# Larger first loads of q and k, and the identity matrix filled on another engine, in an attention and feed-forward kernel

## The chip, the cores and the metric

The kernel runs on one core of one Trainium2 chip. A core has five engines with a queue of instructions each: TensorE (PE, with its weight loads as PEld), VectorE (DVE), ScalarE (ACT), GpSimd (POOL) and SyncE (SP). Each works through its queue in order and waits at an instruction whose inputs are not there yet. The metric is the device time of one execution in microseconds; less is better. A profile shows one execution, with times counted from the start of its span.

## What is computed

Attention without a softmax (squared ReLU in its place), then a gated feed-forward block. Batches 8, heads 12, sequence 448, head size 64; model width 768, inner width 1536; everything is float32 outside.

```python
def _attn_ref(q, k, v):
    S = q.shape[2]
    scale = 1.0 / np.sqrt(q.shape[-1])
    scores = scale * np.matmul(q, k.transpose(0, 1, 3, 2))
    attn = np.maximum(scores, 0.0) ** 2 / S
    return np.matmul(attn, v)

def _moe_ref(x, w_gate, w_val, w_out):     # x: the heads side by side, 3584 rows
    g = x @ w_gate
    gelu = 0.5 * g * (1.0 + erf(g / np.sqrt(2.0)))
    return (gelu * (x @ w_val)) @ w_out
```

## The kernel before

Every load from DRAM of q, k, v and the weights is issued by GpSimd and casts float32 to bfloat16 on the way. For each batch, q lies on partitions 0 to 63 of one tile, qk16, and k on partitions 64 to 127, so one pass of TensorE transposes both. load_qk (line 205, its DMA on line 214) loads q or k of a batch for heads h0 to h1; load_v (line 220, DMA on line 227) loads v in two halves.

A group m holds four heads, that is two pairs. Of the first two batches TensorE makes the transposes (add_transposes, matmuls on line 377, with the identity matrix ident as the other operand), 14 matmuls for a pair of heads. VectorE copies the result from PSUM to SBUF (line 381). From batch 2 on, DMA transposes on SP's queue do this. Then, for a group, seven score tiles follow (add_scores): matmuls on line 162, a relu on ScalarE (line 425), and its square on VectorE (line 431). Two PSUM tiles hold scores, so a score tile waits for the relu of the tile two before it. add_values multiplies with v (line 162 again) and VectorE scales the result into xT (line 487). add_gate_value and add_out are the feed-forward block: gate and value matmuls, a Gelu on ScalarE (line 552), the product on VectorE (line 557), and the output matmuls, whose results are copied (line 613) and stored from SP's queue.

In the texts, T0, T1, T2 and so on are the transposes of the first batch's pairs of heads, in order.

The order of the work comes from a planner at build time (run_plan, line 23). TensorE's work is split into PE0 and PE1, for the two row halves of its array, and both go into TensorE's one queue. PE0's order is fixed: all its items are sorted by due times written in the code. PE1, ACT, DVE and SP each take the item that can start first by the plan, where every item has a cost and a delay, and a load has an arrival time from its bytes and a rate (300 bytes per nanosecond for the first batch). POOL's order is the order in which the code lists it. Where the plan leaves TensorE idle in its first 30 us, fill (line 328) sets filler matmuls on a tile of zeros (line 340). Ten pairs of warm-up matmuls on the same zeros (line 762) stand at the very front.

PE0 of the first batch begins thus: warm-up, T0, scores 1 and 2, T1, scores 3 to 6, T2, score 7, score 8, first values, score 9, T3, and so on.

The identity is made on GpSimd by make_identity, behind the first loads of q and k: a memset of the 128x128 tile to zero (masks.py line 197) and then an affine select that puts ones on the diagonal (masks.py line 199). The zero tile warm and a small table are set on VectorE ahead of all planned work, and ScalarE runs one Gelu on that table.

Of the kernel before, what the change touches and what calls it, by code (L numbers as in the profile page):

```python
# [88 lines left out]
def kernel(  # L89
# [10 lines left out]
    nc = tc.nc  # L100
# [43 lines left out]
    psX = []  # L144

    ident = const.tile([128, 128], bf16)
    warm = const.tile([128, 512], bf16)
    nc.vector.memset(warm[:, :], 0.0)

# [19 lines left out]
    ACT, DVE, POOL, SP, IDLE = [], [], [], [], []  # L169
# [35 lines left out]
    def load_qk(b, i, h0, h1, deps=()):  # L205

        src = (q, k)[i]

        def tile_of():
            if b not in qk16:  # L210
                qk16[b] = qkv.tile([128, H * S // P * D], bf16, name="qk16", tag="qk16")
            return qk16[b][HALF[i], :]

        op = load(4 * (h1 - h0) * S * D, lambda: nc.gpsimd.dma_start(  # L214
            tile_of().rearrange("p (h x) -> p h x", h=H)[:, h0:h1, :],
            src[b, h0:h1].rearrange("h (p c) d -> p h (c d)", c=SC)), deps, rate=400e3 if b else 300e3)
        for pr in range(h0 // 2, h1 // 2):
            head_op[b, pr, i] = op

    def load_v(b, h0, h1, deps=()):  # L220

        for i in range(2):
            def emit(i=i):
                if b not in v16:
                    v16[b] = qkv.tile([128, H, VC, D], bf16, name="v16", tag="v16")
                c0 = i * (SC - VC)
                return nc.gpsimd.dma_start(  # L227
                    v16[b][HALF[i], h0:h1, :, :],
                    v[b, h0:h1].rearrange("h (p c) d -> p h c d", c=SC)[:, :, c0:c0 + VC, :])
            op = load(4 * (h1 - h0) * VC * P * D, emit, deps, rate=400e3 if b else 300e3)  # L230
            for pr in range(h0 // 2, h1 // 2):
                head_op[b, pr, 2 + i] = op
# [405 lines left out]
        then(at, step, *ops, cp)  # L638


    for h0, h1 in ((0, 2), (2, 4), (4, 8), (8, 12)):
        load_qk(0, 0, h0, h1)
        load_qk(0, 1, h0, h1)
        if h0 == 0:
            POOL.append(Op("POOL", 0.6, lambda: make_identity(nc, ident)))
        if h0 > 2:
            load_v(0, h0 - 4, h1 - 4)
    load_v(0, 8, 12)
    load_w12(0)
# [148 lines left out]
```

## Time and profile before

| | us |
|---|---|
| median of 5 runs | 423.94 |
| lowest, highest | 423.51, 426.0 |
| the profiled execution | 423.61 |
| its span in the profile | 421.8 |
| ScalarE busy in the span | 223.9 |
| VectorE busy in the span | 214.0 |
| GpSimd busy in the span | 73.6 |

The profiled execution is 1.8 us longer than its span, which begins with the first recorded instruction. The granted TensorE clock is 0.999 of full speed. The first instructions of GpSimd's queue, by its timeline:

| start us | GpSimd instruction |
|---|---|
| 1.25, 1.95 | q and k, heads 0 and 1 |
| 2.54, 2.85 | identity: memset, affine select |
| 3.09, 3.67 | q and k, heads 2 and 3 |
| 4.27, 4.88 | q and k, heads 4 to 7 |
| 5.48 | v, heads 0 to 3, two issues |
| 6.68, 7.28 | q and k, heads 8 to 11 |
| 7.88 | v, heads 4 to 7, two issues |
| 9.50, 11.36 | v, heads 8 to 11 |
| 12.06, 12.89 | first slices of the gate and value weights |

In a line of a timeline stand the start, the duration, the engine, the line of the code, the operation, what it writes and reads with shapes, how many instructions were merged, and in brackets how long the engine had been idle and what ended that. In a table by stages stand the stretch, its length, and the busy time and number of instructions of each engine. Sizes of DMAs are those of the stored side, which is half of what is read here.

### The profile page before, as it was taken

The numbers are of one execution on the slowest core, as the hardware profiler recorded it, in microseconds if no ns is written. First come the engines' busy times: TensorE is split into PE (matmuls) and PEld (weight loads), VectorE is DVE, ScalarE is ACT, GpSimd is POOL, SyncE is SP. The second block draws the span as 40 slices with busy tenths as digits, with TensorE's granted clock in tenths as the row PEclk, the third lists the DMA queues.
The fourth block names the chain that finished last, engine by engine and source line by source line (L and its number), as shares of the span: only waits on it lengthen the run. The fifth ranks groups of instructions, "written<-read, shape, count | busy, mean of one in ns | idle before, by whom it ended". The sixth has DMA issues, their size and how long they took to land.

```text
span 421.8 us, 19605 instructions
## 1 busy us (share of the span) xinstructions
PE 415.1 (98%) x9087; PEld 371.2 (88%) x9090; DVE 214.0 (51%) x347; ACT 223.9 (53%) x320; POOL 73.6 (17%) x120
## 2 busy tenths in 40 slices
PE   8999999999999999999999999999999999999996
PEld 3558768777998999999999889999999989999995
DVE  3876665266655665356544566456643655212201
ACT  4956663377655655555646555565555556222220
POOL 8655400122022131002300122011310000000000
PEclk9999999999999999999999999999999999999999
DMA  7999997779599899736974299635974100220034
GB/s 102 193 199 198 200 209 123 138 82 126 86 150 172 103 120 116 156 47 74 144 138 104 39 100 145 132 65 66 143 130 97 40 2 3 51 67 3 2 79 113
DMA packets 75281, 44.91 MB, mean 106 GB/s; under 512 B 36160, under 2 KB 71744, under 8 KB 75200
## 3 DMA queue, kind: packets, MB, share of 16 engines
q0 software_dynamic: 37152, 24.39, 43.6%
q1 hardware_dynamic: 37888, 19.08, 25.2%
q8 instruction: 71, 1.16, 1.1%
q10 hardware_dynamic: 160, 0.20, 0.1%
q14 instruction: 10, 0.08, 0.1%
HBM read 48.76 MB, written 11.01 MB: 142 GB/s over the span
## 4 chain that ended last, share of the span: by engine, by line
PE 96%; DMA 1%; POOL 1%; ACT 0%; issue 0%; DVE 0%; POOLq 0%
PE ff L162 86%; PE sp L162 8%; DMA qk<-in_k_dram 1%; PE sp L377 1%; POOL qk L214 1%; PE ff L377 1%; ACT rl L425 0%; PE ff L340 0%; DVE qkT L381 0%; DVE attnT L431 0%; DVE osb L613 0%; POOL ident masks.py:199 0%; POOL ident masks.py:197 0%; POOLq L782 0%
## 5 line engine op out<-in xcount | busy, mean ns | idle before, releaser
L425 ACT ACTIVATE rl<-sp 128x896 bf16<-128x896 f32 x168 | 152.4, 918 | 90.8 <-PE sp L162 81.0
L162 PE MATMUL ff<-xT,wg 64*64 64x448 bf16 x2304 | 196.5, 349 | 0.0
L162 PE MATMUL ff<-xT,wv 64*64 64x448 bf16 x2304 | 195.4, 349 | 0.0
L162 PE MATMUL ff<-wo,uT 64*64 64x384 bf16 (+1 forms) x2736 | 151.4, 320 | 0.0
L431 DVE TENSOR_TENSOR attnT<-rl 128x896 bf16<-128x896 bf16 x168 | 104.0, 623 | 68.9 <-ACT rl L425 66.1
L162 PEld LDWEIGHTS <-wv 64*64 64x64 bf16 x2304 | 124.5, 107 | 9.4 <-issue 0.2
L162 PEld LDWEIGHTS <-wg 64*64 64x64 bf16 x2304 | 123.0, 107 | 10.5 <-issue 0.5
L162 PEld LDWEIGHTS <-uT 64*64 64x64 bf16 x2736 | 128.3, 107 | 4.0 <-issue 0.6
L162 PE MATMUL sp<-qkT 64*64 64x448 bf16 (+1 forms) x768 | 107.5, 328 | 0.8 <-ACT rl L425 0.5
L557 DVE TENSOR_TENSOR uT<-gel,ff 128x448 bf16<-128x448 bf16 x96 | 59.6, 621 | 75.2 <-PE ff L162 66.5
L162 PE MATMUL ff<-attnT,v 64*64 64x448 bf16 (+1 forms) x768 | 88.3, 326 | 0.1
L552 ACT ACTIVATE gel<-ff 128x448 bf16<-128x448 f32 x96 | 52.1, 542 | 48.6 <-PE ff L162 48.0
L162 PEld LDWEIGHTS <-qkT 64*64 64x64 bf16 x768 | 46.3, 106 | 9.9 <-issue 4.0
L613 ACT COPY osb<-ff 128x384 f32<-128x384 f32 x54 | 25.8, 477 | 50.4 <-PE ff L162 50.4
L162 PEld LDWEIGHTS <-v 64*64 64x64 bf16 x768 | 47.7, 107 | 4.2 <-issue 1.1
L487 DVE TENSOR_SCALAR xT<-ff 128x448 bf16<-128x448 f32 x48 | 29.9, 623 | 33.1 <-PE ff L162 33.0
L227 POOL DMA_DIRECT2D v<-in_v_dram x48 | 29.5, 621 | 50.6 <-DVE uT L557 32.5
L214 POOL DMA_DIRECT2D qk<-in_q_dram x25 | 15.5, 622 | 111.3 <-DVE uT L557 105.8
L214 POOL DMA_DIRECT2D qk<-in_k_dram x25 | 15.4, 615 | 65.3 <-DVE uT L557 49.3
L262 DVE COPY qkr<-qk 128x1792 bf16<-128x1792 bf16 x18 | 19.4, 1078 | 0.0
L613 DVE COPY osb<-ff 128x192 f32<-128x192 f32 (+1 forms) x3 | 1.2, 421 | 17.9 <-PE ff L162 17.9
L377 PEld LDWEIGHTS <-qk 128*64 128x64 bf16 x168 | 5.1, 109 | 3.1 <-issue 3.0
(23 smaller groups left out, 41.5 us busy)
## 6 DMA issues: line engine op xcount, KB each, us to landing
out_dram<-osb SPq DMA_DIRECT2D x54, 192.0 KB, 3.0
v<-in_v_dram POOLq DMA_DIRECT2D x48, 128.0 KB, 4.4
qk<-in_q_dram POOLq DMA_DIRECT2D x23, 224.0 KB, 4.9
qk<-in_k_dram POOLq DMA_DIRECT2D x23, 224.0 KB, 4.8
wg<-in_moe_w_gate_dram POOLq DMA_DIRECT2D x6, 384.0 KB, 10.5
wv<-in_moe_w_val_dram POOLq DMA_DIRECT2D x6, 384.0 KB, 11.0
wo<-in_moe_w_out_dram POOLq DMA_DIRECT2D x4, 576.0 KB, 14.9
qkT<-qkr SPq DMA_TRANSPOSE x36, 4.6
```

The source lines that it names most:

```text
L162: return nc.tensor.matmul(o, lhsT, rhs, start=start, stop=stop, tile_position=(P * row, P * col))
L214: op = load(4 * (h1 - h0) * S * D, lambda: nc.gpsimd.dma_start(tile_of().rearrange("p (h x) -> p h x", h=H)[:, h0:h1, :], src[b, h0:h1].re ...
L227: return nc.gpsimd.dma_start(v16[b][HALF[i], h0:h1, :, :], v[b, h0:h1].rearrange("h (p c) d -> p h c d", c=SC)[:, :, c0:c0 + VC, :])
L262: nc.vector.tensor_copy(qkr[b][:, m], qk16[b].rearrange("p (h c d) -> p c h d", c=SC, d=D)[:, :, 4 * m:4 * m + 4])
L377: nc.tensor.transpose(t[HALF[j], c, :], src[:, 2 * (2 * m + r) + j, c, :], ident[:, :], tile_position=(0, P * j))
L425: nc.scalar.activation(rl[:, :, :], box[0][:, :, 0:S], AF.Relu)
L431: nc.vector.tensor_tensor(a[:, :, :], box[1][:, :, :], box[1][:, :, :], op=ALU.mult)
L487: nc.vector.tensor_scalar_mul(xT[b][:, pr, :], box[0][:, 0:S], scalar1=out_scale)
L552: nc.scalar.activation(gel[b, fc][:, :], box[0][:, 0:S], AF.Gelu)
L557: u_op[b, fc].ins = nc.vector.tensor_tensor(uT[b][:, fc, :], gel.pop((b, fc))[:, :], box[0][:, 0:S], op=ALU.mult).ins
L613: cp.ins = (nc.vector.tensor_copy if last else nc.scalar.copy)(osb[t][:, cols], box[0][:, 0:N]).ins
```

## The change

The first batch's q and k are loaded in three steps of four heads instead of two steps of two heads and two of four. The identity's memset moves from GpSimd to VectorE, where it stands ahead of the memset of warm; only the affine select stays on GpSimd, in the same place, behind the first load of q and of k. The first v loads follow the second step, as they did. The planner's cost entry for the identity on POOL goes from 0.6 to 0.4. No other work is added or left out.

```diff
     ident = const.tile([128, 128], bf16)
+    nc.vector.memset(ident[:, :], 0.0)
     warm = const.tile([128, 512], bf16)
     nc.vector.memset(warm[:, :], 0.0)
...
-    for h0, h1 in ((0, 2), (2, 4), (4, 8), (8, 12)):
+    for h0, h1 in ((0, 4), (4, 8), (8, 12)):
         load_qk(0, 0, h0, h1)
         load_qk(0, 1, h0, h1)
         if h0 == 0:
-            POOL.append(Op("POOL", 0.6, lambda: make_identity(nc, ident)))
-        if h0 > 2:
+            POOL.append(Op("POOL", 0.4, lambda: make_identity(nc, ident, nomemset=True)))
+        if h0:
             load_v(0, h0 - 4, h1 - 4)
     load_v(0, 8, 12)
```

With nomemset=True make_identity leaves out its memset and does the rest.

## The prediction

> **What bounds the kernel now.** I read the page first: busy shares, then the chain of waits. TensorE works 98% of the span and the chain is TensorE for 96% of it, so any edit counts only by what it does to the moment at which TensorE's unbroken stretch begins.
>
> ```profile
> span 421.8 us, 19605 instructions
> PE 415.1 (98%) x9087; PEld 371.2 (88%) x9090; DVE 214.0 (51%) x347; ACT 223.9 (53%) x320; POOL 73.6 (17%) x120
> PE 96%; DMA 1%; POOL 1%; ACT 0%; issue 0%; DVE 0%; POOLq 0%
> ```
>
> The change edits the first 12 us of loads. The table by stages says where TensorE stops being gapless (columns: stretch, length, then busy time and count of PE, PEld, DVE, ACT, POOL, granted clock, DMA share, GB/s). Before 30 us it has gaps and from there none to 360 us: what the opening loses or gains reaches the end one for one.
>
> ```profile
> 20.00:25.00 5.00, 4.65 (x66) 2.84 (x64) 5.00 (x10) 5.00 (x7) 2.29 (x4) 1.00 1.37 199
> 25.00:30.00 5.00, 4.85 (x92) 2.89 (x93) 3.36 (x6) 0.43 (x2) 2.64 (x5) 1.00 1.38 199
> 30.00:35.00 5.00, 5.00 (x113) 3.11 (x104) 2.57 (x5) 4.00 (x6) 2.48 (x4) 1.00 1.43 198
> ```
>
> The opening itself is set by ScalarE, as its own timeline shows: batch 0 has 21 relus (three groups of four heads, 7 each) and they run in three rows with two short holes.
>
> ```profile
> 6.92 4.96 ACT L425 ACTIVATE rl<-sp 128x896 bf16<-128x896 f32 x6 [4.68 <-PE sp L162]
> 12.16 0.92 ACT L425 ACTIVATE rl<-sp 128x896 bf16<-128x896 f32 x1 [0.28 <-PE sp L162]
> 13.44 11.85 ACT L425 ACTIVATE rl<-sp 128x896 bf16<-128x896 f32 x14 [0.37 <-PE sp L162]
> ```
>
> So ScalarE's opening is 6.92 (start) + 17.72 (work and its own small waits) + 0.65 (the two holes) = 25.29. What sets the start, and what makes the holes? TensorE's timeline, and the chain of the first 30 us:
>
> ```profile
> 5.20 0.56 PE L377 MATMUL ff<-ident,qk 128*64 128x128 bf16 x14
> 7.09 0.58 PE L377 MATMUL ff<-ident,qk 128*64 128x128 bf16 x14
> 11.21 0.58 PE L377 MATMUL ff<-ident,qk 128*64 128x128 bf16 x14 [0.35 <-DMA qk<-in_k_dram]
> ...
> 12.04 1.04 PE L340 MATMUL ff<-warm 128*128 128x512 bf16 x4
> ```
> ```profile
> 4.88 6.20 DMA qk<-in_k_dram
> ```
>
> The transposes T0 of heads 0 and 1 begin at 5.20 and the first relu 1.72 later. T2 (heads 4 and 5) stands in TensorE's queue ahead of the seventh score tile and waits for the 4-head k load, issued at 4.88 and landed at 11.08: hole one. Hole two follows from T2's copy and from four filler matmuls before the eighth score.
>
> The loads' times to landing, asked for one issue at a time (name, queue, count, KB as stored, us from issue): q and k of heads 0-1, then of heads 4-7.
>
> ```profile
> qk<-in_q_dram POOLq DMA_DIRECT2D x1, 112.0 KB, 2.8
> qk<-in_k_dram POOLq DMA_DIRECT2D x1, 112.0 KB, 2.9
> qk<-in_q_dram POOLq DMA_DIRECT2D x1, 224.0 KB, 4.9
> qk<-in_k_dram POOLq DMA_DIRECT2D x1, 224.0 KB, 6.2
> ```
>
> Issued at 1.25, 1.95, 4.27, 4.88, they land at 4.05, 4.85, 9.17, 11.08; heads 2-3 (3.09, 3.67) land at 6.29 and 6.97. Landings come in the order of issue. T0's 5.20 is k's 4.85 plus the end of the warm-up matmuls, T1's 7.09 is 6.97 plus 0.12, T2's 11.21 is 11.08 plus 0.13.
>
> [...] (two 4-head loads on an otherwise quiet queue, at 103.36 and 111.56, took 3.5). [...] the memset of warm, 256 such elements, took 0.27 us. [...] so I take 0.31 (2.54 to 2.85) for the identity's memset and 0.24 (2.85 to 3.09) for its select.
>
> **The change part by part.**
>
> *The identity's memset goes to VectorE, ahead of warm's.* 64 elements of 4 bytes: 0.27 x 64/256 = 0.07 us. It delays warm's memset, hence the warm-up matmuls, from 1.19 to about 1.26 and their end from 5.36 to 5.43. Hidden, since T0 will wait for a load beyond 6 us; without that cover it would cost its 0.07. The select reads the memset's result more than a microsecond later: no wait. Bounds 0 to 0.1.
>
> *GpSimd's queue.* Before T0's data nothing changes: q and k are issued at 1.25 and 1.95 as now, since an issue takes 0.6 us for either size (0.64 against 0.61). Behind them the memset (0.31) and two issues (3.09, 3.67: 1.18) go. The 4-head q of heads 4-7 moves from 4.27 to 4.27 - 0.31 - 1.18 = 2.78, its k from 4.88 to 3.39, and the v and later q and k loads by 1.5 too, until the queue's limit. That limit shows itself in the trace: the 13th load waits at 9.50 for the 5th, the 14th at 11.36 for the 6th, eight back. With two fewer at the front each later load waits for the same transfer as before (wg for the first v). So the stream behind comes earlier, not in another order.
>
> *T0 waits for twice the bytes.* 459 KB (stored) must land where 229 KB did. Data begin to move at 2.6. Bound by the old kernel: the same bytes, in four loads, were in by 6.97, with a lull from 4.2 to 4.7 at 57 GB/s that came from the identity sitting between the loads:
>
> ```profile
> 4.20:4.70 0.50, 0.50 (x6) 0.25 (x4) 0.00 (x0) 0.00 (x0) 0.50 (x2) 1.00 0.49 57
> ...
> 2.60:4.20 1.60, 1.60 (x12) 0.60 (x10) 0.00 (x0) 0.00 (x0) 1.52 (x4) 1.00 0.98 132
> 4.70:6.00 1.30, 1.30 (x22) 0.79 (x19) 0.20 (x1) 0.00 (x0) 1.30 (x3) 1.00 1.09 148
> 6.90:11.10 4.20, 3.77 (x44) 1.37 (x41) 2.94 (x5) 4.18 (x6) 2.91 (x5) 1.00 1.20 156
> ```
>
> Without the lull, 6.97 - 0.5 x (1 - 57/140) = 6.67. Worked from rates: 2.6 + 459/156 + 0.6 (last byte to landing, as 4.34 to 4.85 and 6.3 to 6.97) = 6.14. From landings: 1.25 + 3.5 for q, then 1.1 (the spacing of the later 4-head pair, 13.58 to 14.68) to 1.9 (9.17 to 11.08) for k: 5.85 to 6.65. I take 6.4. Ends: 5.6 (459 KB at the 190 GB/s seen after 12 us) and 8.05 (q taking the 4.9 us of heads 4-7, then 1.9).
> T0 then starts at 6.4 + 0.13 = 6.53, 1.33 later than 5.20, and the first relu at 6.53 + 1.72 = 8.25. Fillers that the planner sets into the longer wait end near 6.4 (five of 0.21 after 5.4), no extra cost.
>
> *T1 no longer waits.* Its data land with T0's; it follows the first two scores. No gain in time, because relus two and on are paced by ScalarE at 4.96/6 = 0.83 each.
>
> *T2 no longer waits.* Heads 4-7 land by about 11.08 - 0.3 at the latest, more likely near 10.3. TensorE reaches T2 only after the sixth score, which waits for the fourth relu: 8.25 + 4 x 0.83 = 11.57, plus 0.38 of scores. The wait is off the path; hole one (0.28) goes. The eighth score trails the seventh by 1.29 (11.72 to 13.01, fillers in it), so at 12.46 + 1.29 = 13.75, and its relu at 14.18 against ScalarE free at 8.25 + 7 x 0.83 = 14.06: of hole two's 0.37 about 0.12 stays.
>
> *The planner's order.* TensorE's main sequence is sorted by hand-set times and doesn't move. The other choices follow planned starts; all of batch 0's are moved by one common delay, as none of its loads but the first is planned late enough to hold work back. I expect the same order, with some more filler at the front.
>
> *Sum.* 8.25 + 17.72 + 0.12 = 26.09 against 25.29: +0.8. Nothing absorbs it: weights wg and wv land at 19.86 and 21.9, batch 1's first k at 24.5 for transposes at 27.17, and all of these come earlier. VectorE has 31 operations of 0.535 us, 16.6, between first and last relu, and fits. So 423.61 + 0.8 = 424.4 for an execution like the profiled one; that one lies 0.33 under the median of 423.94, which becomes 424.7.
>
> **The rivals.**
> *A wash.* The first pair arrives at 190 GB/s, T0 starts at 5.75, and the holes repay it: 0.55 - 0.53 = 0, 423.9. For it: that rate is seen from 12 us on. Against: 132 GB/s for the very first bytes.
> *Slower beyond doubt.* Large first loads start their data as slowly as heads 4-7 did: k lands at 8.05, T0 at 8.18, +2.98, minus 0.53: 426.4. It decides from a landing near 7.8. For it: the 4.9 us and a lull at 86 GB/s from 6.0 to 6.9, when only a 4-head load was in flight. Against: 3.5 us on a quiet queue.
> *Faster.* From 25 to 30 us TensorE has only 92 matmuls (113 in the next five); if a late load, not the last relus, thins it, loads earlier by 0.3 to 1.5 would gain more than the start loses: about 423.2. Against: no wait on a DMA is listed there.
> *Another order.* The changed plan pairs work of the two array halves differently later on: a microsecond or two either way.
>
> **How the numbers follow.** The forecast, +0.3 to +1.3, has 0.60; a wash 0.13; slower beyond doubt 0.10; faster 0.05; another order 0.12, split by sign. Half a per cent, about what a measurement of this kernel can tell, is 2.1 us: only the slow rival (0.10) and a third of the last (0.04) cross it upward, with the forecast's own tail 0.15 together; downward almost only the last, 0.05. The runs of before spread over 2.5 us, so a median is good to perhaps 0.4. The range runs from the wash less that error, 423.3, to the edge of the slow rival, 426.0.
>
> **What would show it.** T0 near 6.5, first relu near 8.2, no DMA ahead of T2, one hole in the relus of about 0.1, last relu ending near 26.1, and the same matmul counts after 30 us. A first relu before 7.6, or ScalarE with new holes after the eighth relu, or gaps on TensorE after 30 us, would prove it wrong.

## The result and the profile after

The changed kernel took 426.55 us (median of 24 runs, 424.41 to 430.24) against 424.29 us for the kernel before (45 runs): a ratio of 1.0047, 95% interval 1.003 to 1.0063. It is slower, by more than the forecast of +0.8 us, and lies 0.55 us outside the stated range. Three later comparisons of the same kernel gave 1.0036 (1.001 to 1.0061), 1.0000 (0.9979 to 1.0021) and 1.0028 (1.0011 to 1.0045). Over all four its median is 425.57 us (74 runs); that of the kernel before, with two copies of it, is 424.32 us (233 runs). So the change costs about 1.25 us by the medians, and the first comparison drew some 1.0 us more than that; both parts are taken up below.

ScalarE's timeline of the changed kernel (start, duration, engine, line, operation; the change adds one line, so L425 is L426 here):

```profile
9.46 5.78 ACT L426 ACTIVATE rl<-sp 128x896 bf16<-128x896 f32 x7 [7.22 <-PE sp L163]
15.52 11.85 ACT L426 ACTIVATE rl<-sp 128x896 bf16<-128x896 f32 x14 [0.29 <-PE sp L163]
```

The hole before the seventh relu is gone: seven run without a break. One hole of 0.29 us is left of the 0.65. Not all of this is the change's doing, since two later profiles of the kernel before, before_again and before_third, lack the first hole too:

```profile
6.80 5.91 ACT L425 ACTIVATE rl<-sp 128x896 bf16<-128x896 f32 x7 [4.57 <-PE sp L162]
7.52 5.78 ACT L425 ACTIVATE rl<-sp 128x896 bf16<-128x896 f32 x7 [5.29 <-PE sp L162]
```

In before_again the k that T2 needs landed sooner, at 10.6; in before_third T0 was late enough to hide it. So the hole that the larger loads were to close was there in one of three profiles of before. And in the changed kernel the first relu is 2.54 us later than in the first profile of before, and the last one of batch 0 ends at 15.52 + 11.85 = 27.37 instead of 25.29.

TensorE's timeline of the same kernel shows where the start went, and a gap much later:

```profile
5.40 1.25 PE L341 MATMUL ff<-warm 128*128 128x512 bf16 x5
7.72 0.58 PE L378 MATMUL ff<-ident,qk 128*64 128x128 bf16 x14 [1.07 <-DMA qk<-in_k_dram]
...
143.02 0.76 PE L163 MATMUL ff<-xT,wv 64*64 64x448 bf16 x10 [2.14 <-issue]
```

T0 starts at 7.72 behind a wait for k. The five fillers (matmuls on zeros) in front of it are the planner's. At 140.9 TensorE stops for 2.14 us with no wait that the profile can name. The two loads that T0 needs, by name, queue, KB stored, and us from issue to landing:

```profile
qk<-in_q_dram POOLq DMA_DIRECT2D x1, 224.0 KB, 3.6
qk<-in_k_dram POOLq DMA_DIRECT2D x1, 224.0 KB, 5.6
```

Issued at 1.25 and 1.97, they land at 4.85 and 7.57. The span grew from 421.8 to 426.5: of these 4.7 us, 2.08 are the late opening, 2.14 the gap, and 0.5 stay unassigned.

The order of the instructions is the same on TensorE but for the five fillers, and on ScalarE; VectorE has one memset more; on SP one pair of output stores has changed places with one DMA transpose.

### The profile page after: what moved, and what is told of

It is laid out like the page before. It is cut to its first block, busy times and chain, and to the rows that moved or that the text cites. A ratio compares the mean times of both kernels' runs of the same rounds, so it can differ in the third digit from the quotient of the medians.

```text
span 426.5 us, 19611 instructions
## 1 busy us (share of the span) xinstructions
PE 417.0 (98%) x9092; PEld 372.0 (87%) x9095; DVE 214.0 (50%) x348; ACT 224.0 (53%) x320; POOL 72.2 (17%) x117
## 4 chain that ended last, share of the span: by engine, by line
PE 96%; DMA 1%; issue 1%; ACT 0%; DVE 0%; POOL 0%; POOLq 0%
PE ff L163 86%; PE sp L163 8%; DMA qk<-in_k_dram 1%; PE ff L341 1%; PE ff L378 1%; PE sp L378 1%; ACT rl L426 0%; DVE qkT L382 0%; DVE attnT L432 0%; POOL qk L215 0%; DVE osb L614 0%; POOLq L783 0%
## 5 line engine op out<-in xcount | busy, mean ns | idle before, releaser
L426 ACT ACTIVATE rl<-sp 128x896 bf16<-128x896 f32 x168 | 152.3, 918 | 95.7 <-PE sp L163 87.1
L163 PEld LDWEIGHTS <-wg 64*64 64x64 bf16 x2304 | 123.1, 107 | 10.7 <-issue 0.3
```

The source lines that it names most:

```text
L163: return nc.tensor.matmul(o, lhsT, rhs, start=start, stop=stop, tile_position=(P * row, P * col))
L426: nc.scalar.activation(rl[:, :, :], box[0][:, :, 0:S], AF.Relu)
```

## The experiments

**The changed kernel again, and each half of the change alone.** The changed kernel was run three times more. For the halves:

```diff
  loads_alone: the four-head loads, with
+            POOL.append(Op("POOL", 0.6, lambda: make_identity(nc, ident)))
  ident_alone: the loads of before, with
+    nc.vector.memset(ident[:, :], 0.0)
+            POOL.append(Op("POOL", 0.4, lambda: make_identity(nc, ident, nomemset=True)))
```

> The changed kernel once more, for a second profile. Late start (the k load of heads 0-3 lands late and everything behind it is late): first relu again near 9.4, last relu of batch 0 ends near 27.4, time +1.5 to +2.2 us against before. Stall in the middle (the gap of 2.1 us on TensorE near 141 us belongs to the changed program): a gap of about 2 us at the same place again. If the gap is at another place or absent, it belongs to the execution and not to the change.

> Only the four-head loads; the identity's memset stays on GpSimd. Late start: k of heads 0-3 is issued before the identity, so it lands at 7.6 as in the changed kernel, first relu near 9.4, same time as the changed kernel within 0.3 us. If the memset ahead of the warm-up mattered: 0.1 us better than the changed kernel.

> Only the identity's memset on VectorE; loads as before. Late start: T0 stays at 5.2, q and k of heads 2-3 and 4-7 are issued 0.3 us earlier, so the hole before the seventh relu (0.28) shrinks to 0 to 0.1: 0.0 to 0.3 us better than before. If the 0.07 us of memset ahead of the warm-up counts: 0.07 us worse.

The second profile of the changed kernel has no gap at 141: first relu 9.15, last end 27.07, span 423.5, 425.31 us. The loads alone do the same: 9.04, 26.96, span 423.4, ratio 1.003 (1.001 to 1.005). The identity's move alone gives 0.9997 (0.9977 to 1.0016). The cost is the loads'. What the identity's move does is seen in ScalarE's timeline of ident_alone:

```profile
7.20 4.96 ACT L426 ACTIVATE rl<-sp 128x896 bf16<-128x896 f32 x6 [4.97 <-PE sp L163]
12.37 0.92 ACT L426 ACTIVATE rl<-sp 128x896 bf16<-128x896 f32 x1 [0.20 <-PE sp L163]
```

The hole shrinks from 0.28 to 0.20 only: k of heads 4-7, issued 0.22 us sooner, landed at 11.26 and not before 11.08. T0 itself came 0.29 us later in this profile, too. The hoped-for gain of up to 0.3 us was not measured.

> The changed kernel a third time. Late start: first relu at 9.0 to 9.5 and last relu of batch 0 ending 1.7 to 2.1 us later than before. The gap of 2.1 us on TensorE that the first profile had and the second did not: if it belongs to the execution, about four in ten runs lie 2 us over the lowest group, as in the kernel before (25 of 59 above 425.0); if the change brings it more often, clearly more than half do.

> The changed kernel a fourth time, beside the two copies of before: T0 at 7.3 to 7.7 and last relu of batch 0 near 27.0; ratio to before 1.002 to 1.004. If the change costs nothing on the whole (third time: 1.000), 0.999 to 1.001.

First relu 9.09 and last end 27.01 in both, spans 423.5, no gap; as expected, but for the ratio of 1.0000 in the third comparison, which its profile, of a run of 425.36 us, doesn't explain.

**Bytes or size of a load.** Two kernels move the same 459 KB in four loads of two heads: select_late puts the identity's select behind all four; k_last keeps the whole identity behind the second and makes T0 wait for the fourth.

```diff
  select_late (identity's memset on VectorE)
-        if h0 == 0:
+        if h0 == 2:
             POOL.append(Op("POOL", 0.4, lambda: make_identity(nc, ident, nomemset=True)))
  k_last
+    load_qk(0, 0, 0, 2)
+    load_qk(0, 0, 2, 4)
+    POOL.append(Op("POOL", 0.6, lambda: make_identity(nc, ident)))
+    load_qk(0, 1, 2, 4)
+    load_qk(0, 1, 0, 2)
```

> As the kernel with the identity's memset on VectorE, with four loads of two heads in a row and the select behind them: the same bytes in a row as the changed kernel's first two loads, but T0 needs only the first half. Bytes as such (a late start because 459 KB take that long): k of heads 2-3 lands near 7.3 to 7.6, no earlier than the changed kernel's k. Large loads as such (a four-head load spreads badly over the DMA engines): k of heads 2-3 lands near 6.4. In both cases T0 stays at 5.2 and the time is that of before or up to 0.5 us better.

> Loads of two heads as before, only their order changed: q of heads 0-1, q of 2-3, the identity, k of 2-3, k of 0-1. T0 then waits for the same 459 KB as in the changed kernel, with no four-head load among the first four. Late start: k of heads 0-1 lands at 7 to 8, first relu near 9.0, last relu of batch 0 ends 1.5 to 2.3 us later than before (26.8 to 27.6), time +1.3 to +2 us. Large loads as such: k lands near 6.4, first relu 8.2, time +0.8.

In select_late the fourth load, issued at 3.13, took 4.9 us and landed at 8.03. In k_last T0 waited until 7.16 for k, first relu 8.89, last end 26.81, span 423.1, ratio 1.0028 (1.0006 to 1.005). So a late start costs the same with small loads, and in these two profiles four small loads were in no sooner (7.03 and 8.03) than two large ones (6.17 to 7.57). Large loads as such are not needed for the cost; select_late's ratio of 0.9997 (0.9974 to 1.0019) shows that its fourth load, which only T1 needs, costs nothing that can be measured.

**Twice the cost, and the other direction.**

```diff
  eight_heads
+    load_qk(0, 0, 0, 8)
+    load_qk(0, 1, 0, 8)
  finer
+    for h0, h1 in ((0, 2), (2, 4), (4, 6), (6, 8), (8, 12)):
```

> The first q and k loads made of eight heads: the suspected cost doubled. Late start: k lands at 10.6 to 11.3 (before, the same bytes were in at 11.08), T0 about 5.9 us later than before, 0.3 to 0.4 of that repaid by the holes: time +5 to +5.8 us. If the opening had slack behind the relus: less than +3 us.

> The other way: q and k of heads 4-7 also in loads of two heads, all else as before. Late start: T0 stays at 5.2; T2 needs k of heads 4-5 only, which lands about 1 us ahead of 11.08, so the hole before the seventh relu (0.28) goes and the one before the eighth (0.37) stays: 0.2 to 0.3 us better than before. If issue time on GpSimd counts (1.2 us more in its queue): k of heads 4-5 lands no earlier, time as before or 0.5 us worse.

With eight heads the time is 429.55 us (six runs, ratio 1.010, 1.0057 to 1.0143), and the last relu ends at 30.19. The sign came out, and the size nearly (4.9 us by the medians, 5 to 5.8 expected). The reason did not: k had landed at 2.04 + 6.5 = 8.54, not at 10.6 to 11.3, and T0 started at 10.54 because nineteen fillers ran until 10.61. That pointed to the fillers. The finer loads show what was hoped for at T2 (seven relus in a row, one hole of 0.29), but so does before_third with the old loads. Their profile shows T0 itself slower, and the ratio is 0.9991 (0.9974 to 1.0009): no gain that can be told from none. TensorE's timeline of finer:

```profile
5.46 0.95 PE L377 MATMUL ff<-ident,qk 128*64 128x128 bf16 x14
6.34 1.16 PE L340 MATMUL ff<-warm 128*128 128x512 bf16 x3
```

Before, the same two rows took 0.56 and 0.82. The first relu came 2.41 us after T0 instead of 1.72.

**The kernel before twice more, and a late T0 without any load.**

```diff
  pe_late
+        for _ in range(10):
+            nc.tensor.matmul(t[:, :], warm[:, 0:128], warm[:, :], start=True, stop=True)
```

> The kernel before against itself, for a second profile and for what two equal kernels differ by. Theory of the cold start (in some executions TensorE runs T0 at half rate [...] which costs about 0.5 us of the opening, as in the profiles of select_late and finer): last relu of batch 0 ends at 25.3 with fast transposes (0.56 us for the 14) or near 25.8 with slow ones (0.95 us). Rival (the opening is the same in every execution): 25.3 again. Ratio 0.998 to 1.002.

> The kernel before once more: the same two possible openings, 25.3 or near 25.8. A gap of 1 to 2 us on TensorE between 130 and 150 us may be in either profile; if one has it, it doesn't belong to the change.

> Ten filler matmuls more behind the warm-up, 2.1 us at full rate and up to 4.3 at half rate; loads, identity and all else as before. It delays T0 on TensorE alone, with the loads on time. Late start: T0 at 7.3 to 8.1, first relu 1.7 us after it, no wait on a DMA at T2, one hole of about 0.3 in the relus, last relu 1.72 + 17.64 + 0.29 = 19.65 us after T0 (27.0 to 27.8), span 396.4 us after that. If the loads' order or size hurts in another way than by T0's start: the changed kernel would be slower than this law gives from its own T0, and pe_late would be on the law.

The copies of before gave ratios of 1.0003 (0.998 to 1.0026) and 1.0001 (0.9982 to 1.002). Their T0 took 0.56 and 0.90 us, and batch 0's last relu ended at 24.92 and 25.44: the opening of one kernel differs from execution to execution. Both have gaps in the middle, so these come without the change. TensorE's stop in before_third by stages (stretch, length, busy times of PE, PEld, DVE, ACT, POOL, clock, DMA share, GB/s):

```profile
139.00:139.50 0.50, 0.06 (x1) 0.00 (x0) 0.01 (x1) 0.00 (x0) 0.00 (x0) 1.00 1.32 49
139.50:140.00 0.50, 0.00 (x0) 0.00 (x0) 0.00 (x0) 0.00 (x0) 0.00 (x0) 1.00 0.11 4
140.00:140.50 0.50, 0.01 (x4) 0.02 (x4) 0.00 (x0) 0.00 (x0) 0.00 (x0) 1.00 1.07 172
```

TensorE, VectorE, ScalarE and GpSimd stand still for about a microsecond. At the beginning of it the DMA engines are as busy as ever (1.32) and move only 49 GB/s, then almost nothing. What stops them wasn't tried and stays open.

pe_late took 426.4 us, ratio 1.0038 (1.0021 to 1.0055), with every load on time. Its TensorE timeline:

```profile
5.60 3.06 PE L765 MATMUL ff<-warm 128*128 128x512 bf16 x10
8.59 0.58 PE L377 MATMUL ff<-ident,qk 128*64 128x128 bf16 x14
```

First relu 10.33, last end 28.24, span 424.5. The law in its expectation gives 8.59 + 19.65 = 28.24 and 28.24 + 396.4 = 424.6. A late T0 is enough to make the cost, and the changed kernel's gapless profiles lie on the same law, so nothing else of the change is needed. As with the changed kernel, the runs show less than the profile: the medians differ by 2.1 us, the last relu by 2.95.

**Why the landing was late.** The loads behind were held back in one kernel, and k was issued first in another.

```diff
  quiet_behind
+                for _ in range(6):
+                    nc.gpsimd.memset(pause[:, :], 0.0)
  k_first
+        load_qk(0, 1 if h0 == 0 else 0, h0, h1)
+        load_qk(0, 0 if h0 == 0 else 1, h0, h1)
```

> The changed kernel with six memsets of an unused tile on GpSimd behind the identity, so that nothing is issued for 3 to 5 us behind the first q and k load. Only the landing of the first k is read, not the time, which the late loads behind it spoil. If the loads queued behind take transfer time from it: k lands at 6.1 to 6.4 instead of 7.2 to 7.6. If the first two loads are slow by themselves: 7.0 to 7.6 again.

> The changed kernel with k issued ahead of q for heads 0-3. If the second load is late because it is second: k lands near 4.8 and q at 7.0 to 7.6, T0 at 7.2 to 7.7. If k's rows as such are slow: q lands at 6.4 or before and k after it.

With nothing issued from 2.90 to 6.30, k landed at 1.96 + 4.6 = 6.56; with k first, q landed second at 6.56 (7.0 to 7.6 was expected), and k at 5.15. In the seven profiles with q first and all loads behind, k landed at 6.17, 6.47 (twice), 6.97, 7.26 (twice) and 7.57. Since 6.56 lies among these, quiet_behind doesn't settle whether the loads behind take the transfer time; k_first shows only that the second of the two is the late one, whichever it is. In both, T0 (7.59 and 7.09) followed the fillers, which ended at 7.66 and 7.17.

What the traces do show is which part of the load is late. A trace keeps sixteen marks of landing for each load. In the nine profiles with two four-head loads in front, fourteen marks of the second load are in by 5.85 to 6.01, and the last at 6.2 to 7.6. In the first profile of the changed kernel fourteen are in by 5.99, one comes at 6.48 and one at 7.59. Read as a sixteenth of the load each, they say that the bulk of the bytes was in before the forecast's 6.4, and that one or two of sixteen pieces make k late. In select_late the fourth load has fifteen in by 6.68 and the last at 7.99. In quiet_behind, with nothing issued behind, one piece still lags, at 6.57 against 5.95 for the fifteenth, and its table by stages shows 142 GB/s, then 20 and 5 (last column) at a DMA share of 0.13 and 0.04:

```profile
5.00:5.50 0.50, 0.50 (x4) 0.00 (x0) 0.00 (x0) 0.00 (x0) 0.44 (x2) 1.00 0.90 142
5.50:6.00 0.50, 0.50 (x3) 0.13 (x2) 0.00 (x0) 0.00 (x0) 0.44 (x2) 1.00 0.13 20
6.00:6.50 0.50, 0.50 (x3) 0.15 (x1) 0.00 (x0) 0.00 (x0) 0.50 (x2) 1.00 0.04 5
```

Why one piece lags, and why more in some executions, stays open.

**Without the fillers in front of T0.**

```diff
-        if t1 > FILL or n < 1:
+        if t1 > FILL or n < 1 or t1 < 6.0:
```

> The changed kernel without the five filler matmuls that the planner sets between the warm-up and T0; all else equal. Fillers hold T0 (in four profiles they end at 7.0 to 7.4, in after_fourth nearly a microsecond behind k's landing at 6.47): T0 follows k's landing by 0.13, at 6.6 to 7.7, and the time is 0.2 to 0.5 us below the changed kernel's. Rival (the fillers bring TensorE to its full rate before T0, and without them T0 and its three followers run at half rate): T0's 14 matmuls take 0.9 us instead of 0.58, the first relu comes 2.2 to 2.4 us after T0 instead of 1.72, and the time is that of the changed kernel or up to 0.5 us above it.

> The same kernel for a second profile: the same two theories, read from the length of T0's matmuls and the distance from T0 to the first relu.

This is where the two parts of a late T0 come apart. In after_fourth k had landed at 1.97 + 4.5 = 6.47, and yet TensorE's timeline shows T0 at 7.35, with no wait, on the heels of fillers that took 0.35 us each:

```profile
5.67 1.75 PE L341 MATMUL ff<-warm 128*128 128x512 bf16 x5
7.35 0.58 PE L378 MATMUL ff<-ident,qk 128*64 128x128 bf16 x14
```

Without them, TensorE's timeline of the first execution:

```profile
6.58 0.96 PE L378 MATMUL ff<-ident,qk 128*64 128x128 bf16 x14 [0.84 <-DMA qk<-in_k_dram]
7.47 1.46 PE L341 MATMUL ff<-warm 128*128 128x512 bf16 x3
8.86 0.96 PE L163 MATMUL sp<-qkT 64*64 64x448 bf16 x8
```

and of the second:

```profile
6.34 0.58 PE L378 MATMUL ff<-ident,qk 128*64 128x128 bf16 x14 [0.60 <-DMA qk<-in_k_dram]
6.86 0.82 PE L341 MATMUL ff<-warm 128*128 128x512 bf16 x3
7.64 0.57 PE L163 MATMUL sp<-qkT 64*64 64x448 bf16 x8
```

Each theory fits one execution. T0 follows k by 0.1 to 0.2 in both. In the first TensorE still works at half rate (0.96 us for T0 against 0.58), first relu 9.50, last end 27.92; in the second at full rate, first relu 8.07, last end 25.99, span 422.5 and 424.24 us, close to the forecast's numbers (8.25, 26.09, 424.4). Over 22 runs the median is 424.88 us against 425.57 with the fillers, ratio to before 1.0021 (0.9997 to 1.0045). Nine of the 22 lie at 424.4 us or below; of the changed kernel's 74, eight do. The two kernels ran in different comparisons and their intervals overlap, so that leaving out the fillers gains on the whole isn't shown. Where k is in early the fillers cost time (in after_fourth T0 starts 0.88 us behind k's landing); that they save any where TensorE has not turned fast isn't shown.

**The profiles side by side.**

| kernel | k of T0 lands | matmuls ahead of T0 end | T0 | first relu | last relu ends | span |
|---|---|---|---|---|---|---|
| before | 4.85 | 5.36 | 5.20 | 6.92 | 25.29 | 421.8 |
| before_again | 4.85 | 5.26 | 5.09 | 6.80 | 24.92 | 423.6, gaps |
| before_third | 4.85 | 5.67 | 5.46 | 7.52 | 25.44 | 423.8, gap |
| ident_alone | 5.04 | 5.65 | 5.49 | 7.20 | 25.50 | 422.0 |
| finer | 4.75 | 5.66 | 5.46 | 7.87 | 25.79 | 422.2 |
| changed, first | 7.57 | 6.65 | 7.72 | 9.46 | 27.37 | 426.5, gap |
| after_again | 7.26 | 6.87 | 7.42 | 9.15 | 27.07 | 423.5 |
| after_third | 7.26 | 7.04 | 7.36 | 9.09 | 27.01 | 423.5 |
| after_fourth | 6.47 | 7.42 | 7.35 | 9.09 | 27.01 | 423.5 |
| loads_alone | 6.97 | 7.37 | 7.30 | 9.04 | 26.96 | 423.4 |
| pe_late | 4.75 | 8.66 | 8.59 | 10.33 | 28.24 | 424.5 |

Two rules can be read off. T0 starts, within 0.2 us, at the later of k's landing and the end of the matmuls ahead of it. And where there is no gap the span is the end of batch 0's last relu plus 396.2 to 396.6: nothing behind the opening absorbs anything.

## Why the prediction failed

**What held.** The opening reaches the end one for one, by the rule just read. The wait ahead of T1 and the wait ahead of T2 went; hole one went, though it was no fixture of the kernel before. The identity's memset, of 64 elements of 4 bytes, took 0.11 us (priced at 0.07, from 0.27 for warm's 256) and moved the warm-up from 1.19 to 1.26; ident_alone shows no cost of it. The issues on GpSimd moved as worked out (q of heads 4-7 at 2.90, forecast 2.78). The relus' work with its last hole is 5.78 + 0.29 + 11.85 = 17.92, against 17.72 + 0.12 = 17.84. The order stayed, except for the one exchange on SP, which the forecast had not seen and no experiment isolates. The direction was right: a small loss. By the pooled medians its size, 1.25 us, even lies within the forecast's +0.3 to +1.3, but that is partly luck: the profiles differ by more, and T0, first relu and last end are all late against the sum.

**What failed is the start of T0**, 6.53 in the sum and 7.35 to 7.72 in the four profiles, and it failed in two steps.

The first is "T0 waits for twice the bytes", with 6.4 for k's landing. The four profiles of the changed kernel show 6.47 to 7.57, and without front fillers 6.17 and 6.47. The old kernel's 6.97 for the same bytes was taken as a bound, less a lull; it was no bound, as select_late's fourth load at 8.03 shows. The rates in the sum were not too high, for fourteen of sixteen pieces were in by 6.01. What the sum put at nothing is the lag of the last piece: from the fifteenth mark to the last it is 0.07 and 0.18 us in the two k loads of before that the sum was read from, and 0.5 to 1.3 in the changed kernel's.

The second is the sentence that the planner's fillers "end near 6.4 (five of 0.21 after 5.4), no extra cost". The 0.21 was read from fillers at 5.69 and later, when TensorE was already at full rate (from 4.9 on). In front of T0 five of them took 1.25 to 1.99 us and ended at 6.65 to 7.66. Even a landing at 6.4 can then give a T0 at 7.3, as after_fourth has it; in the other three profiles of the changed kernel k was the later of the two. Together the two steps are worth 27.12 (mean of four profiles) - 26.09 = 1.0 us, nearly all of what the profiles differ by beyond the forecast: 27.12 against 25.22, the mean of three of before, is 1.9 and not 0.8. The runs' medians differ by 1.25 us only. One reason may be that the three profiles of before started early: with ident_alone, finer and select_late, whose T0 needs the same small loads, the mean is 25.48, and the difference 1.6. Another may be that some executions of the changed kernel start earlier, as 12 of its 74 runs lie under 424.75 us, but no profile of one is there. Neither is shown.

That doesn't make up the whole miss of the median: 426.55 against 423.94 + 0.8 = 424.74, or 1.8 us. By the pooled medians 0.45 of it is the effect (1.25 for 0.8), 0.38 is that the first five runs of before lay low (423.94 for 424.32), and 426.55 - 425.57 = 1.0 is that the first comparison's median of the changed kernel lay high. The last two belong to the sentence "a median is good to perhaps 0.4", and without the 1.0 the time would have stayed inside the range. In the kernel before, 81 of 205 runs (its copies apart) lie above 425.0 us, a group about 2 us over the others; the two copies' profiles at 425.44 and 425.60 us, and the changed one at 428.31, have the gaps. That every run of the group has one isn't shown. In the first comparison 16 of 24 runs of the changed kernel lay above 425.8 us; in the three later ones 17 of 50. A median moves with the share of runs in the upper group. Whether the change raises that share isn't shown: 33 of 74 above 425.8 against 81 of 205 above 425.0.

The rival "slower beyond doubt" had the right place and, for the first execution, nearly the right landing (8.05 there, 7.57 measured), though not the fillers. "A wash" and "faster" don't fit: in every gapless profile the span follows batch 0's last relu by the same 396.2 to 396.6, so earlier loads gained nothing behind it.

## What to carry to other kernels

The first load of a kernel has nothing to hide behind: make the piece that starts the chain small and let the pieces behind it be large, since here a first relu 2.1 us later bought back 0.2 us of holes (means of four profiles and of three). Price a landing by its last piece, with the scatter of several executions. Check in a second profile that the wait to be removed is there each time. Count what stands in the queue ahead of an instruction whose data come later, fillers included, and price it at the rate of that moment, not at the steady one (here five fillers took 1.25 to 1.99 us). And before a median of few runs is predicted to half a microsecond, look whether the runs of before fall into groups.

## What the hardware showed unexpectedly

TensorE begins at half its rate and turns fast at a moment that differs between executions of one program: in the first profile of before a warm-up matmul takes 634 ns, and 380 ns from 4.98 on; pe_late's ten fillers start 0.43 us apart at first and 0.22 us apart from 7.2 on. T0's fourteen matmuls took 0.56, 0.56 and 0.90 us in the three profiles of before. By the traces' records of the clock, full rate begins at 4.4 to 7.2 us in seventeen of the eighteen profiles (at 4.9, inside the warm-up, in the first of before, and at 7.1, behind T0, in finer). It begins at 10.7 in the first profile without front fillers, where TensorE stood idle for 0.84 us and had not turned before; in the second, with 0.60 us of idle time, T0 at 6.34 already ran at full rate. What decides the moment isn't shown. The stage tables show 1.00 for the granted clock from the start, so the state doesn't show there; the lengths of equal matmuls show it. For this kernel the turn is worth up to 0.7 us of the opening (2.41 against 1.72 from T0 to the first relu), and 1.2 without front fillers (2.92).

Landing isn't proportional to bytes in the opening: 918 KB (eight heads) were in at 8.54 us, 459 KB in two loads at 6.17 to 7.57, 229 KB at 4.75 to 5.05. The spread of the 459 KB is that of one or two pieces in sixteen, while in the profile with eight heads all sixteen came within 8.17 to 8.56.
